# A recurrent attention kernel: the tail tokens' projections move from one batched stage into the steps, and the reloaded weight pieces change places in each group

## The chip, the core and the metric

The kernel runs on one core of one Trainium2 chip. The metric is the device time of one execution in microseconds (us). The core has five engines that run beside each other: TensorE (PE, matrix products; its weight loads appear as PEld), VectorE (DVE), ScalarE (ACT), GpSimd (POOL) and SyncE (SP, which only issues transfers). Weights come from the chip's memory (HBM) through 16 DMA engines into the on-chip memory SBUF; PE writes its results to eight banks of PSUM.

## What is computed

A sequence of 2048 tokens of width 1024 is cut into 64 segments of 32 tokens. Segment after segment, 8 memory tokens are put in front, the 40 tokens pass through attention with 32 heads of width 128, and the first 8 rows of the result are the memory of the next segment. So the segments form a chain. A gated feed-forward network works on all tokens, and a gate g mixes both.

```python
def _A_ref(x, mem0, Wq, Wk, Wv, Wo, seg_len):
    ...
    mem = mem0
    for s in range(n_seg):
        xs = x[:, s * seg_len:(s + 1) * seg_len, :].copy()
        h = jnp.concatenate([mem, xs], axis=1)
        q = jnp.einsum('btd,dhe->bhte', h, Wq)
        k = jnp.einsum('btd,dhe->bhte', h, Wk)
        v = jnp.einsum('btd,dhe->bhte', h, Wv)
        scores = jnp.einsum('bhqe,bhke->bhqk', q, k) * scale
        scores = jnp.where(mask[None, None], scores, -1000000000.0)
        p = _softmax(scores, axis=-1)
        o = jnp.einsum('bhqk,bhke->bhqe', p, v)
        o = jnp.einsum('bhte,hed->btd', o, Wo)
        mem = o[:, :M, :].copy()
        outs.append(o[:, M:, :])
...
g = _sigmoid((x * gate_w).sum(-1, keepdims=True))
b = _gelu(x @ w_gate) * (x @ w_up) @ w_down
return g * a + (1 - g) * b
```

## The kernel before

**Stages.** A first stage prepares tokens and projects the tail tokens; 64 steps follow, one a segment; then the output projection of the tail tokens (L854 to L874) and the feed-forward network (from L876), neither of which changes.

**Front and tail tokens.** A segment has 8 memory tokens and 32 new ones. A step puts the 8 memory tokens and the first 24 new ones (`NR = 24`) into one tile `hT` of 32 columns. The other 8 (`NB = 8`), the *tail tokens*, do not depend on the chain, so their q, k and v can be computed ahead. Before the change the first stage does so for all 512 tail tokens at once (L481 to L545): their transposed rows `xrT` go against all of Wk, Wq and Wv in products of 512 columns, and the results go to the scratch tensors `qk_scr` and `v_scr` in HBM. Each step reads its part back: `qkr` (L474) twice, once for each half of the heads, and `vB` (L478) once; `put_rest` (L777) copies `qkr` beside the front tokens in `kT` and `qT`.

**Weights.** Wq, Wk, Wv and Wo are 64 pieces of 512 KB: matrix m, half r of the heads, and i = 0 to 7. SBUF has 50 slots (`sl`) for them, so 36 pieces stay and 14 slots are *paired*: the two halves' pieces of the same m and i share one slot (`PAIRS`, L301: 3 for k, 3 for q, 4 for v, 4 for o). When a step has used the piece of one half, `spent` (L354) has SP fetch the other half's piece (L347), which the same step needs later. The next step takes the halves in the other order, so it starts with the pieces that are there. That is 14 fetches, 7.34 MB, in each step.

**A step** (L784 to L849) walks through eight groups of eight pieces in the order k0, q0, v0, k1, q1, o0, v1, o1 (`ORDER`, L293), where 0 is the half taken first. Within a group the pieces go in the order 0 to 7. `proj` (L749) issues 4 products of 128x512 for a piece of k, q or v (L758) and 8 of 128x256 for a piece of o (L770). What else happens is written into the same order by `on(...)`, by group and place: ACT copies a group's PSUM bank out (`evac`, L663), PE transposes it (`trans`, L670), `scores` (L689) and the softmax on DVE and ACT follow, `attend` (L720) multiplies with v, and its results `oT` feed the pieces of o. At the end of a step ACT copies the bank of o to `a_bf` (L832), PE transposes it (L836), and DVE writes the new memory tokens into the next `hT` (L839), after which the next step's k0 can start. `hT` has two buffers, and the next one's new tokens are loaded at place 5 of k0 (L808).

**Who orders what.** Each engine works off its own list in the order of the code, and waits are on semaphores. All fetches are in SP's list, all small reads and stores of the steps in POOL's.

Of the kernel before, what the change touches and what calls it, by code (L numbers as in the profile page):

```python
# [195 lines left out]
def bass_gated_mix__memory_aug_recurrent_mem_tr__geglu_ffn__prompt_kernel(  # L196
# [34 lines left out]
    with ExitStack() as es:  # L231
# [6 lines left out]
        NRT = NSEG * NB  # L238
        NBK = (NRT + 127) // 128
# [3 lines left out]
        qk_scr = nc.dram_tensor("qk_scr", [128, NSEG, 4, 128], BF16)  # L243
        v_scr = nc.dram_tensor("v_scr", [NSEG, NB, 16, 2, 128], BF16)
# [23 lines left out]
        hT = [al(f"hT{i}", [128, KC, 32]) for i in range(2)]  # L268
# [8 lines left out]
        vA = al("vA", [128, 4, 128], at=tok.off)  # L277
# [5 lines left out]
        a_bf = al("a_bf", [128, 256], at=oT.off)  # L283
# [7 lines left out]
        QUADS = (("k", 0), ("q", 0), ("k", 1), ("q", 1), ("v", 0), ("v", 1))  # L291
        pos = [(m, r, kc) for m, r in QUADS for kc in range(KC)] + [("o", r, i) for r in range(2) for i in range(8)]
        ORDER = (("k", 0), ("q", 0), ("v", 0), ("k", 1), ("q", 1), ("o", 0), ("v", 1), ("o", 1))  # L293
        walk = [(m, r, i) for m, r in ORDER for i in range(8)]
        assert len(pos) == 64

        def at_step(p, s):
            m, r, i = (pos if s < 0 else walk)[p]
            return (m, r ^ (s % 2), i)

        PAIRS = {"k": (1, 3, 5), "q": (0, 2, 5), "v": (0, 2, 4, 6), "o": (0, 2, 4, 6)}  # L301
# [12 lines left out]
        for s_ in [-1] + list(range(NSEG)):  # L314
            for p in range(48 if s_ < 0 else 64):
                k = at_step(p, s_)
                if s_ < 0 and k[0] == "v" and paired(k) and k[1] == 1:
                    continue
                uses[home[k]].append(k)
# [48 lines left out]
        for g in range(4):  # L368
# [11 lines left out]
        xrT = al("xrT", [128, KC, NRT])  # L380
        stq = [al(f"stq{i}", [128, max(NSEG, 64), 128]) for i in range(2)]
        xq = [al(f"xq{i}", [128, 4, KC, SEG]) for i in range(2)]
        assert cur[0] <= top

        tmpv = {k: al(f"tmpv{k[2]}", [128, 2048], at=stq[0].off + PIECE * n)
                for n, k in enumerate(("v", 1, i) for i in PAIRS["v"])}
        assert len(tmpv) * PIECE <= 2 * stq[0].nb
        cur[0] = slots[home["v", 0, 0]].off
        px = [al(f"px{i}", [128, D]) for i in range(min(NT, 16))]
        gwb = al("gwb", [128, D])  # L390
        gp = al("gp", [128, D], FP32, at=kT.off)
# [34 lines left out]
        for b in range(NBK):  # L426
# [6 lines left out]
            if b + 2 < NBK:  # L433
                rest_t.append(load_rest(b + 2))
# [553 lines left out]
```

## Time and profile before

| | us |
|---|---|
| three runs, median (lowest to highest) | 2736.53 (2732.96 to 2737.52) |
| the profiled execution's own time | 2737.58 |
| its span, first to last instruction | 2735.8 |
| PE busy over the span | 2236.5 (82%) |
| DVE / ACT / POOL busy | 900.9 / 540.3 / 437.9 |
| HBM traffic | 611.60 MB read, 30.41 MB written |

A row of a table by stretches gives the stretch, each engine's busy time with its number of instructions, the TensorE clock that was granted (1.00 is full speed), the mean busy share of the 16 DMA engines, and what they moved in GB/s. A row of the list of waits names the waiting instruction, whom it waited for, the total, how often, and the longest. A row of a timeline has start, length, engine, line, operation, output and inputs, shape, count, and in brackets the idle time before it with what ended it. A row of the DMA issues has the number of transfers, the size of each, and the median time from issue to landing. Instructions of one kind that follow each other are merged in a timeline.

### The profile page before, as it was taken

The numbers are of one execution on the slowest core, as the hardware profiler recorded it, in microseconds if no ns is written. First come the engines' busy times: TensorE is split into PE (matmuls) and PEld (weight loads), VectorE is DVE, ScalarE is ACT, GpSimd is POOL, SyncE is SP. The second block draws the span as 40 slices with busy tenths as digits, with TensorE's granted clock in tenths as the row PEclk, the third lists the DMA queues.
The fourth block names the chain that finished last, engine by engine and source line by source line (L and its number), as shares of the span: only waits on it lengthen the run. The fifth ranks groups of instructions, "written<-read, shape, count | busy, mean of one in ns | idle before, by whom it ended". The sixth has DMA issues, their size and how long they took to land.

```text
span 2735.8 us, 71514 instructions
## 1 busy us (share of the span) xinstructions
PE 2236.5 (82%) x32250; PEld 1046.5 (38%) x32294; DVE 900.9 (33%) x2089; ACT 540.3 (20%) x1129; POOL 437.9 (16%) x931
## 2 busy tenths in 40 slices
PE   7896777777777777777777777777878999999998
PEld 3442333333333333333333333333335444444443
DVE  1422233232333233323323333233230544445262
ACT  1211111121211121212112112112120312213030
POOL 1401222222122221222212212212210000000000
PEclk9998988899888899988888888889799999999999
DMA  8678787787877778878778787778788343250705
GB/s 307 181 209 318 253 280 267 262 293 251 293 270 264 278 260 282 282 252 285 263 258 285 256 286 281 242 275 283 241 293 288 131 150 112 85 177 15 247 1 200
DMA packets 293745, 646.78 MB, mean 236 GB/s; under 512 B 76728, under 2 KB 87992, under 8 KB 293440
## 3 DMA queue, kind: packets, MB, share of 16 engines
q1 hardware_dynamic: 237040, 594.63, 61.3%
q0 software_dynamic: 15360, 25.29, 3.8%
q10 hardware_dynamic: 41040, 22.29, 2.8%
q8 instruction: 254, 4.16, 0.6%
q14 instruction: 51, 0.42, 0.1%
HBM read 611.60 MB, written 30.41 MB: 235 GB/s over the span
## 4 chain that ended last, share of the span: by engine, by line
PE 49%; DMA 39%; DVE 5%; ACT 3%; issue 2%; SPq 1%; ACTq 1%; POOL 1%; POOLq 0%
DMA sl<-in_A_Wq_dram 23%; PE pb L758 14%; DMA sl<-in_A_Wo_dram 13%; PE pb L905 12%; PE pb L770 7%; PE pb L942 6%; PE pb L673 2%; PE pb L864 2%; PE pb L529 2%; PE pb L501 2%; DMA wd<-in_B_w_down_dram 2%; ACT tok L656 1%; ACT a_bf L656 1%; SPq L347 1%; PE pb L836 1%
## 5 line engine op out<-in xcount | busy, mean ns | idle before, releaser
L758 PE MATMUL pb<-sl,hT 128*32 128x512 bf16 x12288 | 905.2, 422 | 211.1 <-DMA sl<-in_A_Wk_dram 96.5
L758 PEld LDWEIGHTS pb<-sl,hT 128*32 128x32 bf16 x12288 | 309.7, 101 | 603.2 <-issue 159.9
L770 PE MATMUL pb<-sl,oT 128*32 128x256 bf16 x8192 | 346.6, 311 | 78.4 <-DMA sl<-in_A_Wo_dram 49.3
L770 PEld LDWEIGHTS pb<-sl,oT 128*32 128x32 bf16 x8192 | 223.4, 107 | 155.0 <-issue 91.3
L656 ACT ACTIVATE tok<-pb 128x512 bf16<-128x512 f32 x256 | 153.4, 599 | 397.7 <-PE pb L758 392.7
L905 PE MATMUL pb<-xT,wg 128*128 128x512 bf16 x896 | 211.8, 380 | 8.4 <-DVE GT L921 8.4
L741 POOL COPY oRc<-oT 128x128 bf16<-128x128 bf16 x128 | 96.0, 750 | 764.3 <-DVE oT L659 764.3
L905 PE MATMUL pb<-xT,wu 128*128 128x512 bf16 x896 | 211.7, 379 | 0.0
L942 PE MATMUL pb<-wd,GT 128*128 128x512 bf16 x876 | 193.9, 380 | 9.5 <-DMA wd<-in_B_w_down_dram 8.3
L659 DVE COPY kT<-pb 128x512 bf16<-128x512 bf16 x128 | 54.4, 425 | 337.8 <-PE pb L673 309.7
L659 DVE CAST oT<-pb 128x160 bf16<-128x160 f32 x256 | 71.3, 320 | 263.6 <-PE pb L732 263.6
L656 ACT ACTIVATE oT<-pb 128x160 bf16<-128x160 f32 x256 | 63.8, 301 | 425.0 <-PE pb L732 425.0
L704 ACT ACTIVATE E<-pb 128x320 bf16<-128x320 f32 x128 | 55.9, 437 | 417.9 <-DVE pb L703 417.9
L905 PEld LDWEIGHTS pb<-xT,wg 128*128 128x128 bf16 x896 | 86.8, 98 | 116.5 <-DVE GT L921 12.8
L942 PEld LDWEIGHTS pb<-wd,GT 128*128 128x128 bf16 x896 | 86.7, 98 | 116.7 <-DMA wd<-in_B_w_down_dram 13.2
L913 ACT ACTIVATE s<-pb 128x512 f32<-128x512 f32 x112 | 66.8, 596 | 323.0 <-PE pb L905 303.5
L727 PE MATMUL pb<-tA,vA 32*128 32x40 bf16 x2048 | 37.3, 185 | 112.7 <-DVE tB L717 112.7
L905 PEld LDWEIGHTS pb<-xT,wu 128*128 128x128 bf16 x896 | 87.5, 98 | 105.8
L914 DVE SCALAR_TENSOR_TENSOR tp<-s,pb 128x512 f32<-128x512 f32 x112 | 77.0, 687 | 136.7 <-ACT s L913 136.6
L501 PE MATMUL pb<-xrT,sl 128*128 128x512 bf16 x499 | 117.1, 390 | 5.2 <-DMA sl<-in_A_Wq_dram 2.5
L673 PE MATMUL pb<-ident,tok 128*128 128x128 bf16 x1024 | 111.6, 238 | 8.9 <-ACT tok L656 2.6
L673 PEld LDWEIGHTS pb<-ident,tok 128*128 128x128 bf16 x1024 | 63.6, 104 | 136.1 <-ACT tok L656 121.3
(76 smaller groups left out, 1821.3 us busy)
## 6 DMA issues: line engine op xcount, KB each, us to landing
sl<-in_A_Wv_dram SPq DMA_DIRECT2D x268, 512.0 KB, 11.4
sl<-in_A_Wo_dram SPq DMA_DIRECT2D x268, 512.0 KB, 6.4
sl<-in_A_Wk_dram SPq DMA_DIRECT2D x208, 512.0 KB, 7.1
sl<-in_A_Wq_dram SPq DMA_DIRECT2D x208, 512.0 KB, 9.5
wd<-in_B_w_down_dram SPq DMA_DIRECT2D x56, 1024.0 KB, 5.7
qk_scr<-stq ACTq DMA_DIRECT2D x4, 2048.0 KB, 18.3
qkr<-qk_scr POOLq DMA_DIRECT2D x128, 64.0 KB, 4.8
wg<-in_B_w_gate_dram SPq DMA_DIRECT2D x3, 1792.0 KB, 15.9
```

Of the source, the lines that this page charges most:

```text
L501: ins = e.matmul(PB[b][:, 0:NRT], lhsT=w8[kc][:, c:c + 128], rhs=xrT[:, kc, :], start=(kc == 0), stop=(kc == KC - 1))
L656: op("act", lambda e: e.activation(o, i, ACTF.Copy), rd=rd, wr=wr)
L659: op("dve", lambda e: e.tensor_copy(o, i), rd=rd, wr=wr)
L673: ins = e.transpose(PBV[TT][:, j * 128:(j + 1) * 128], tok[:, j * 128:(j + 1) * 128], ident[:, :])
L704: op("act", lambda e: e.activation(E8[:, :, :].rearrange("p a c -> p (a c)"), PB[SS][:, 0:320], ACTF.Exp, scale=scale), rd=[BK(SS)], wr=[E ...
L741: op("pool", lambda e: e.tensor_copy(oRc[:, :, 16 * u:16 * u + 16].rearrange("p c x -> p x c"), oT[:, :, :, 32:40].rearrange("p g j c -> p ...
L758: ins = e.matmul(PB[bk][32 * g:32 * g + 32, :], lhsT=h[:, i, :], rhs=w[:, g * 512:(g + 1) * 512], start=(i == 0), stop=(i == KC - 1))
L770: ins = e.matmul(PB[XO][32 * g:32 * g + 32, 0:256], lhsT=oT[:, gp_, 2 * jj + hh, 0:32], rhs=w[:, c:c + 256], start=(r == 0 and i == 0 and ...
L905: ins = e.matmul(PB[bk][:, 0:FB], lhsT=w[:, kc, cc:cc + 128], rhs=xT[:, :, :, kc, :].rearrange("p t i c -> p (t i) c"), start=(kc == 0), s ...
L913: op("act", lambda e, hg=hg: e.activation(s1[:, :], hg, ACTF.Square, scale=SQ), rd=[BK(bg)], wr=[s1.r()])
L914: op("dve", lambda e, hg=hg, t=t: e.scalar_tensor_tensor(out=t[:, :], in0=s1[:, :], scalar=1.0, in1=hg, op0=ALU.add, op1=ALU.mult), rd=[BK ...
L942: ins = e.matmul(PB[bank[2 * k + hf]][:, :], lhsT=GT[:, j, tb * 128:(tb + 1) * 128], rhs=w[:, jj, hf * 512:(hf + 1) * 512], start=(j == 0) ...
```

## The change

The batched stage is gone. The first stage now only transposes the tokens, 16 tiles of 128, and writes beside `xq_scr` a second scratch `xr_scr` with the tail tokens of each group of four segments: 4 x 8 = 32 columns, as many as `hT` has. The tile `hR` holds one such group. A *fill* is the projection of a group's 32 tail tokens with one half of Wk, Wq or Wv: eight pieces of 4 products, as in a step. A group of four segments needs six fills, and in four consecutive steps two, two, one and one of them are done for the group ahead (table `FILL`). They use pieces that are in their slots at that time, so they fetch no weights. The results go to `qk_scr` and `v_scr`. Step 0 does the fills of group 0 itself, as its pieces arrive, and one of group 1.

```diff
-        hT = [al(f"hT{i}", [128, KC, 32]) for i in range(2)]
+        hT = al("hT", [128, KC, 32])
+        hR = al("hR", [128, KC, 32])
-        vA = al("vA", [128, 4, 128], at=tok.off)
+        vA = al("vA", [128, 4, 128], at=oT.off)
-        a_bf = al("a_bf", [128, 256], at=oT.off)
+        a_bf = al("a_bf", [128, 256], at=qT.off)
+        stage = {n: al(n + "S", [128, 512], at=t.off) for n, t in (("k", kT), ("q", qT), ("o", oT))}
+        def seq(m, r):
+            p = [i for i in range(8) if i in PAIRS[m]]
+            f = [i for i in range(8) if i not in p]
+            return p + f if r == 0 else f + p
-        walk = [(m, r, i) for m, r in ORDER for i in range(8)]
+        walk = [(m, r, i) for m, r in ORDER for i in seq(m, r)]
...
+            if T > 0:
+                op("act", lambda e: e.dma_start(xr_scr[T], to.rearrange("p k i c -> p (k i c)")),
...
+        def fill(m, u, b, h=hR):
+            ks = [(m, u, i) for i in range(8)]
...
+                    for g in range(4):
+                        ins = e.matmul(PB[b][32 * g:32 * g + 32, :], lhsT=h[:, k[2], :], rhs=w[:, g * 512:(g + 1) * 512],
+                                       start=(n == 0), stop=(n == 7))
...
+        def fill_evac(m, u, G, b, st):
+            st = stage[st]
+            if m == "v":
+                act_copy(st[:, :], PB[b][:, :], [BK(b)], [st.r()])
+                for g in range(4):
+                    op("pool", lambda e, g=g: e.dma_start(
+                        v_scr[4 * G:4 * G + 4, :, 4 * g:4 * g + 4, u, :].rearrange("s i j c -> (s i) j c"),
...
+            else:
+                act_copy(tok[:, :], PB[b][:, :], [BK(b)], [tok.r()])
+        def fill_put(m, u, G, st):
+            if m == "v":
+                return
...
+                    ins = e.transpose(PBV[TT][:, j * 128:(j + 1) * 128], tok[:, j * 128:(j + 1) * 128], ident[:, :])
...
+            op("pool", lambda e: e.dma_start(qk_scr[:, 4 * G:4 * G + 4, m4, :], st[:, :].rearrange("p (i y) -> p i y", i=4)),
+               rd=[st.r()], wr=[("D", "qk", G, m4)], lane="fq")
...
+        FILL = ((("k", 1), ("q", 1)), (("q", 0), ("v", 0)), (("v", 1),), (("k", 0),))
...
-            on("k", 0, 5, lambda: load_h(s + 1) if not last else None)
+                on("k", 0, 5, lambda: load_v(s))
-            on("v", 0, 7, lambda: scores())
+            on("k", 1, 0, lambda: scores())
-            on("q", 1, 4, lambda: attend(ua))
+                on("q", 1, 5, lambda: attend(ua))
-            on("o", 0, 7, lambda: scores())
+            on("v", 1, 0, lambda: scores())
+            two = len(fl) > 1
+            n1, n2, n3 = (3, 3, 8) if two else (0, 3, 2)
+            on("v", 1, 0, some(f1, n1))
+            on("o", 1, 0, lambda: load_h(s + 1) if not last else None)
             on("o", 1, 0, lambda: evac(bko["v", 1], vA, "act"))
+            on("o", 1, 0, some(f1, n2))
             on("o", 1, 0, lambda: attend(ub))
-            on("o", 1, 0, lambda: load_v(s + 1) if not last else None)
+            on("o", 1, 0, some(f1, n3))
+            on("o", 1, 0, o_store)
...
             act_copy(a_bf[:, :], PB[XO][:, 0:256], [BK(XO)], [a_bf.r()])
+            fb = f2 if two else f1
+            run(fb, 4 if two else 2)
...
+            run(fb)
```

`seq` puts a group's paired pieces first in the half taken first and last in the half taken second. Three memory places are shared anew: `vA` no longer lies on `tok` but on `oT`, `a_bf` on `qT`, and the staging tiles of the fills (`kS`, `qS`, `oS`) on `kT`, `qT` and `oT`.

The change moves rows on **PE at the end of a step** and the start of the next one. `sl` tiles are weight pieces with their slot numbers (the numbers of before are two or three lower), `oT`, `hT`, `hR` the tokens' side of a product, `pb` a PSUM bank. Before, from the middle of o1 to the third piece of k0 of the next step:

```order
L770 MATMUL pb<-sl_113,oT 32x256 x8
L770 MATMUL pb<-sl_114,oT 32x256 x8
L770 MATMUL pb<-sl_116,oT 32x256 x8
L770 MATMUL pb<-sl_117,oT 32x256 x8
L836 MATMUL pb<-ident,a_bf 128x128 x2
L758 MATMUL pb<-sl_69,hT_53 32x512 x4
L758 MATMUL pb<-sl_71,hT_53 32x512 x4
L758 MATMUL pb<-sl_72,hT_53 32x512 x4
```

Now, the same place in a step with two fills:

```order
L674 MATMUL pb<-sl_119,oT 32x256 x8
L689 MATMUL pb<-sl_85,hR 32x512 x4
L689 MATMUL pb<-sl_87,hR 32x512 x4
L689 MATMUL pb<-sl_88,hR 32x512 x4
L689 MATMUL pb<-sl_90,hR 32x512 x4
L836 MATMUL pb<-ident,a_bf 128x128 x2
L689 MATMUL pb<-sl_92,hR 32x512 x4
L689 MATMUL pb<-sl_93,hR 32x512 x4
L689 MATMUL pb<-sl_95,hR 32x512 x4
L689 MATMUL pb<-sl_97,hR 32x512 x4
L662 MATMUL pb<-sl_74,hT 32x512 x4
L662 MATMUL pb<-sl_77,hT 32x512 x4
```

Four pieces of the second fill now stand between the last piece of o and the transposes of `a_bf`, and four between these and k0 (two and one in a step with one fill). The last piece of o is a paired one (`sl_119`), where it was an unpaired one (`sl_117`), and k0 begins with a paired one (`sl_74`), where it was an unpaired one (`sl_69`).

On **POOL**, from the last `oRc` copy of a step to the first memset of the next, the small transfers change places. Before:

```order
L741 COPY oRc<-oT 128x16x8
L478 DMA vB<-v_scr 128x1x256
L778 COPY kT<-qkr 128x16x8
L778 COPY qT<-qkr 128x16x8
L845 DMA a_scr<-a_bf 4x32x256
L847 DMA o_scr<-oRc 128x256
L474 DMA qkr<-qk_scr 128x256
L469 DMA hT_53<-xq_scr 128x256
L701 MEMSET pB 128x144
```

Now, behind a step with two fills, whose second is one of v:

```order
L433 DMA hT<-xq_scr 128x256
L646 COPY oRc<-oT 128x16x8
L817 DMA o_scr<-oRc 128x256
L719 DMA qk_scr<-kS 128x4x128
L846 DMA a_scr<-a_bf 4x32x256
L700 DMA v_scr<-oS 32x4x128 x4
L723 COPY kT<-qkr 128x16x8
L723 COPY qT<-qkr 128x16x8
L442 DMA qkr<-qk_scr 128x256
L446 DMA vB<-v_scr 128x1x256
L606 MEMSET pB 128x144
```

The load of `hT` and the store of `oRc` moved ahead of the step's end, the load of `vB` behind the start of the next step, and the fills' stores (`qk_scr`, `v_scr`) came in.

On **SP** at the start of the program the token tiles 8 to 15 (`px`, whose buffers are used a second time) now stand ahead of the Wv pieces:

```order
L351 DMA sl_94<-in_A_Wq_dram 128x2048
L351 DMA sl_96<-in_A_Wq_dram 128x2048
L403 DMA px_122<-in_A_x_dram 128x1024
L403 DMA px_123<-in_A_x_dram 128x1024
L403 DMA px_124<-in_A_x_dram 128x1024
L403 DMA px_125<-in_A_x_dram 128x1024
L403 DMA px_126<-in_A_x_dram 128x1024
L403 DMA px_127<-in_A_x_dram 128x1024
L403 DMA px_128<-in_A_x_dram 128x1024
L403 DMA px_129<-in_A_x_dram 128x1024
L351 DMA sl_98<-in_A_Wv_dram 128x2048
```

Before, each tile had a buffer of its own, and their loads stood between the pieces of the first two groups.

More of the change, by code (lines that the diff above doesn't have):

```diff
@@ L383, in bass_gated_mix__memory_aug_recurrent_mem_tr__geglu_ffn__prompt_kernel @@
+        dl = al("dl", [128, NT], FP32)
         assert cur[0] <= top
[L385 to L391, printed above, removed]
-        pr = [al(f"pr{i}", [128, D], at=kT.off + 2048 * i) for i in range(2)]
```

330 lines of the change are left out of this document (150 added, 180 removed).

## The prediction

> **What bounds the kernel now.** I first read the table by stretches, cut at the start of the wait for step 0's first reloaded piece, at the end of step 0, and at the end of the last step.
>
> ```profile
> 0.00:219.50 219.50, 190.87 (x1059) 90.02 (x1077) 62.31 (x96) 42.35 (x72) 40.67 (x43) 0.97 0.75 238
> 219.50:248.60 29.10, 16.10 (x301) 6.87 (x301) 4.88 (x14) 3.47 (x9) 3.67 (x9) 0.69 0.86 325
> 248.60:2080.00 1831.40, 1400.24 (x28009) 657.22 (x28011) 557.47 (x1575) 354.71 (x821) 393.60 (x879) 0.88 0.78 272
> 2080.00:2736.00 656.00, 629.31 (x2883) 292.35 (x2906) 276.26 (x404) 139.78 (x228) 0.00 (x0) 1.00 0.38 132
> L656 ACT ACTIVATE a_bf<-pb x64: 383/383/384, 248.2 to 2062.2; 128x256 bf16<-128x256 f32 x64
> ```
>
> The first stage is PE's: 190.87 of 219.50 us busy. In the steps neither PE (1400 of 1831 us) nor the DMA engines (0.78) are full. `a_bf` ends each step: 64 of them, the first at 248.2, the last at 2062.2, so a step takes 1814.0/63 = 28.79 us. Behind the last `a_bf` lie 2737.58 - 2062.6 = 675.0 us that the change leaves alone.
>
> Next the list of PE's waits within the steps:
>
> ```profile
> PE pb L727 <- DVE tB L717: 110.9, 63, 1.8
> PE pb L758 <- DMA sl<-in_A_Wq_dram: 92.0, 122, 2.8
> PE pb L758 <- DMA sl<-in_A_Wk_dram: 83.4, 104, 2.2
> PE pb L770 <- DMA sl<-in_A_Wo_dram: 49.3, 82, 2.2
> PE pb L836 <- ACT a_bf L656: 30.5, 63, 0.5
> PE pb L770 <- ACT oT L656: 26.8, 63, 0.4
> PE pb L758 <- DVE hT L839: 17.9, 63, 0.3
> ```
>
> More than half is for fetched pieces: 224.7 us, 3.6 a step. The rest, 186 us, is the chain of the data: softmax, the copies of `oT`, the end of a step. To see whether the fetches wait in a full queue or come late, I cut one step, from its k0 to the next k0:
>
> ```profile
> 1051.77:1054.00 2.23, 2.23 (x44) 1.15 (x48) 0.00 (x0) 0.27 (x1) 2.03 (x4) 1.00 0.30 85
> 1054.00:1068.00 14.00, 11.39 (x213) 4.27 (x205) 4.75 (x13) 3.25 (x8) 1.58 (x5) 0.88 0.99 353
> 1068.00:1074.00 6.00, 4.15 (x122) 2.58 (x118) 3.35 (x9) 1.22 (x3) 0.73 (x2) 1.00 0.85 278
> 1074.00:1078.00 4.00, 2.40 (x68) 1.30 (x68) 0.56 (x2) 0.50 (x2) 1.58 (x4) 0.87 0.66 248
> 1078.00:1080.29 2.29, 1.44 (x19) 0.68 (x19) 0.19 (x1) 0.38 (x1) 0.44 (x1) 0.50 0.00 0
> ...
> 1094.00:1096.00 2.00, 0.73 (x28) 0.28 (x24) 0.56 (x2) 0.99 (x3) 1.03 (x2) 1.00 1.03 420
> ```
>
> The DMA engines are full for 14 us (0.99, 353 GB/s), dip while the pieces of o are asked for, and stand still at the end of the step. So a step is one long queue of 14 pieces, then a tail in which nothing can be fetched because nothing has been used yet. (The last row is two of the best microseconds of the step after it.) The timeline of the same step shows both ends:
>
> ```profile
> 1052.43 1.30 SPq L347 DMA_DIRECT2D sl<-in_A_Wk_dram  x3
> 1067.80 3.49 SPq L347 DMA_DIRECT2D sl<-in_A_Wo_dram  x4
> 1051.77 2.77 PE L758 MATMUL pb<-sl,hT 128*32 128x512 bf16 x48 [0.28 <-DVE hT L839]
> 1054.48 0.40 PE L673 MATMUL pb<-ident,tok 128*128 128x128 bf16 x4
> 1068.57 1.06 PE L770 MATMUL pb<-sl,oT 128*32 128x256 bf16 x32
> 1070.24 1.93 PE L758 MATMUL pb<-sl,hT 128*32 128x512 bf16 x32
> 1078.08 1.05 PE L770 MATMUL pb<-sl,oT 128*32 128x256 bf16 x16 [0.47 <-DMA sl<-in_A_Wo_dram]
> 1079.61 0.40 PE L836 MATMUL pb<-ident,a_bf 128*128 128x128 bf16 x2 [0.49 <-ACT a_bf L656]
> 1080.29 4.46 PE L758 MATMUL pb<-sl,hT 128*32 128x512 bf16 x48 [0.28 <-DVE hT L839]
> ```
>
> 48 products are 12 pieces: 2.77/12 = 0.231 us a piece at clock 1.00, and 4.46/12 = 0.372 us where the clock was half; a piece of o takes 1.06/4 = 0.27, four transpositions 0.40.
>
> **The change, part 1: the start of the program.** The batched projections go, and with them a first stage as long as PE's work. What remains before `a_bf` of step 0 is loading. I count what must land before step 0 can leave its fills: 38 pieces of k, q and v, 12 of o and the 10 reloaded ones of k, q and v, 60 x 0.524 = 31.5 MB; tokens in 4.2 MB, their transposed form out 4.2, the tail tokens' scratch 1.0, the rest (gate vector, seven fills' stores, small reads) 1.6: 42.4 MB. At the full queue's 353 GB/s that is 120.1 us.
>
> ```profile
> pr<-in_A_x_dram SPq DMA_DIRECT2D x4, 256.0 KB, 3.7
> sl<-in_A_Wv_dram SPq DMA_DIRECT2D x268, 512.0 KB, 11.4
> qk_scr<-stq ACTq DMA_DIRECT2D x4, 2048.0 KB, 18.3
> qkr<-qk_scr POOLq DMA_DIRECT2D x128, 64.0 KB, 4.8
> DMA to landing us min/median/max: 3.5/8.5/15.7
> DMA to landing us min/median/max: 2.9/5.8/7.8
> L456 POOL TENSOR_TENSOR gp<-px,gwb 128x1024 f32<-128x1024 bf16 x16 | 34.0, 2123 | 82.8 <-DVE dl L458 63.5 <-DMA px<-in_A_x_dram 19.3
> L458 DVE TENSOR_REDUCE dl<-gp 128x1 f32<-128x1024 f32 x16 | 19.5, 1218 | 15.8 <-POOL gp L456 15.8
> ```
>
> (The two rows without a name are those of the weight pieces and of `hT`.) In front come 3.7 us until a first tile lands. Behind come the k1 and q1 pieces, a transposition and the first piece of o, 16 x 0.231 + 0.40 + 0.27 = 4.4 us; then the four last pieces of o, asked for only now: 3.5 us for one alone (the least of the first unnamed row) and 3 x 0.524/0.353 = 4.5 us for the others; then 0.7 us. Sum: 3.7 + 120.1 + 4.4 + 8.0 + 0.7 = 136.9 us, against 248.6 at the end of step 0's `a_bf` before: **-111.7 us**. The gate's pass (2.12 us on POOL, then 1.22 on DVE, one tile after the other, 16 x 3.4 = 54 us) holds the SP list at tiles 8 to 15 until about 36 us; until then 16 pieces and 15 tiles, 12 MB, are under way with 3 MB of stores, 42 us of queue, so I cost it at nothing; without that cover it is 10 us. The fills' round trips through HBM (some 10 us from store to `qkr`, at twice 4.8) lie under the same queue. Bounds: 118 us at the 420 GB/s of the best row, and 157 at step 0's own 325 GB/s with the 10 us.
>
> **Part 2: one step.** Per step, against 28.79:
> - First fetch after one piece of k0 instead of two: -0.23.
> - The dip: SP needs 3.49 us for the o fetches because the pieces 0, 2, 4, 6 lie between others; now all four are first. At 0.85 of 6 us the dip is worth 0.9: -0.9, between 0 and 1.4 (with part of the next row).
> - At the end one piece of o, not two, stands behind the last landing: -0.3 (half of 1.05 at half clock, 0.26 at full).
> - The load of `hT` and the store of `oRc` leave the first microseconds, in which the k pieces ask for the engines, and go beside the o pieces; `vB` comes in. Two transfers of 64 KB at 353 GB/s are 0.4: -0.4, between 0 and -1.0.
> - The fills' stores and `hR`: (6 x 128 + 64) KB for four steps, 0.213 MB a step, in pieces of 256 bytes. At 353 GB/s 0.6 us of the full queue; at the pace of the one row with such pieces, 2048 KB in 18.3 us, 1.85. That row's transfers shared the queue with weights, so I take +0.85, nearer the low end.
> - The tail: with two fills, 4 pieces stand where PE waited 0.49 for `a_bf`, and 4 where it waited 0.28 for `hT`: +1.07 at full clock, +2.21 at half. With one fill (2 and 1 pieces) it is 0 to +0.35. Half of the steps have two: +0.7, between 0.55 and 1.3.
> - All other fill pieces (8 or 5 ahead of o1) lie in the wait for `tB` (1.76 a step), that for `oT` (0.43) and that for o pieces. In a step with one fill 3 x 0.231 cover part of `tB` only. Their four transpositions (of k and q) for four steps, 0.40 each, fall in waits for pieces. 0, as long as the o pieces land last; without that cover up to 1.85.
> - `hT` with one buffer: its load may start when the last v1 product has read it, 1072.17 in this step, 8.1 us before the next k0; it lands in 5.8 and DVE and its semaphore take 0.5. 0, with 1.8 us to spare.
> - `vB`, issued some 5 us into a step, is needed at the fifth piece of q1, where q pieces are waited for anyway: 0.
>
> Sum: -0.23 - 0.9 - 0.3 - 0.4 + 0.85 + 0.7 = **-0.28 a step**, 63 x 0.28 = 17.6 us. All terms at their ends: -2.0 to +2.4.
>
> So PE receives 96 fills x 8 x 0.231 = 177 us of work, nearly what the first stage had, and the steps hardly grow, since the 431 us in which PE stood still take it, while the queue of fetches stays as long.
>
> Sum against the profiled execution: 2737.58 - 111.7 - 17.6 = **2608 us**. The median of the three runs is 1 us below that execution, which I leave out.
>
> On the granted clock: 0.88 over the steps, 0.50 in the last row of the step. The Trainium skill, "TensorE: Matmul & The Clock Gate", section "Why this matters for your kernels", says that idle gaps of PE of more than about 3 us put it back to half clock; the trace agrees in kind, since half clock comes here behind the stretches of waits, although the longest single wait in the list is 2.8 us. By that rule the fills would keep PE warm, and its 1400 us at 0.88 would be 1232 at 1.00. I give this no term, because a step ends with a fetch and not with PE; it is part of the first rival's chance.
>
> **The rivals.**
> - *The queue has slack that only PE's order kept it from using.* For it: 0.70, 0.15 and 0.34 of the first, third and fourth stretch are idle. Against: the 14 us at 0.99. It gives the favourable ends of all terms, -2.0 a step: 2737.58 - 111.7 - 126 = 2500.
> - *The stores in 256-byte pieces and half-clock fills in the tail eat the gain.* For it: 18.3 us for 2 MB, and half clock in the last row. Against: 18.3 was measured in a shared queue. With +1.85 for the stores a step is 0.72 longer than before: 2608 + 63 x 1.0 = 2671. The Trainium skill, "DMA: Bandwidth & Descriptors", section "Specifications", wants at least 512 B a transfer for line rate and says that smaller ones are read, modified and written. That speaks against moving these stores into the stage where the queue is the limit. The 18.3 us agree with a slow store but can't tell that cause from queueing.
> - *Slower than before: `hT` lands too late.* Its load now competes with four pieces of o, and with it waits the whole next step. In favour: Wv pieces, queued behind others, take 11.4 us; against: a 64 KB load on POOL's own queue never took over 7.8. Each us beyond 7.6 is a us of every step. From 1.8 + 0.28 = 2.1 us more, a landing after 9.7, the gain of the start is gone; at 11.4 it is 63 x 3.8 = 239 more: 2847.
> - *The change doesn't do what it says at the start,* since loads hold each other up as they did in the first stage (238 GB/s over it): 42.4 MB then take 178 us, 58 more: 2666.
>
> **How the numbers follow.** Forecast (steps between 1.1 shorter and 0.3 longer than before) 0.50; queue with slack 0.17; slow stores 0.19; `hT` late 0.06; long start 0.08. Range: the first stage's -19 and +20 with steps 1.2 shorter and 1.1 longer than forecast, not added in full: 2512 to 2700. It leaves out most of the first rival, the third, and the worst of the second. A measurement of this kernel tells 0.2% (5 us) from no change. Faster by more than that: 0.93, all cases but the third rival and a rest; within: 0.01; slower: 0.06.
>
> **What would show it.** Right: the first `a_bf` ends near 137; the distance of `a_bf` is about 28.5, longer in steps with two fills than in those with one; the wait for `tB` is mostly gone, and PE's waits for DMA move to o1; the dip in the DMA share closes; PE busy in the steps rises by some 180 us. Wrong: DVE's copy into `hT` waits for the transfer of `hT`; the DMA share in the steps stays at 0.78 while steps get shorter or longer; or the first `a_bf` is past 157.

## The result and the profile after

| | before | after |
|---|---|---|
| median of 4 runs (lowest to highest), us | 2734.74 (2716.38 to 2737.52) | 2508.94 (2505.66 to 2514.83) |
| ratio, 95% interval | | 0.919 (0.9145 to 0.9235) |
| the profiled execution's own time / span, us | 2737.58 / 2735.8 | 2514.83 / 2512.9 |

The changed kernel takes 8.1% less time. The table by stretches of its profile, cut where step 0's last fetches are asked for, and at the ends of the first and of the last `a_bf`, and the row of `a_bf`:

```profile
0.00:110.00 110.00, 38.96 (x461) 21.77 (x465) 35.48 (x67) 15.95 (x28) 44.89 (x49) 0.90 0.99 378
110.00:138.30 28.30, 22.04 (x413) 10.69 (x409) 5.61 (x15) 5.50 (x11) 9.04 (x17) 0.84 0.36 115
138.30:1843.80 1705.50, 1416.97 (x31012) 731.06 (x31004) 582.12 (x1633) 410.72 (x907) 532.49 (x1073) 0.97 0.83 296
1843.80:2513.00 669.20, 641.37 (x2944) 298.44 (x2944) 276.12 (x404) 140.38 (x230) 0.73 (x1) 0.99 0.40 138
L561 ACT ACTIVATE a_bf<-pb x64: 384/384/386, 137.9 to 1843.4; 128x256 bf16<-128x256 f32 x64
```

The first `a_bf` ends at 138.3 instead of 248.6: 110.3 us less. From there to the last one are 1705.5 us instead of 1814.0, so a step takes (1843.4 - 137.9)/63 = 27.07 us instead of 28.79: 63 x 1.72 = 108.5 us less. What lies behind the last `a_bf` is 669.1 us instead of 673.2. These three make up the whole 222.9 us between the spans. So the two halves of the gain are alike in size, and the second was forecast at 17.6.

PE's waits in the steps (from 139 to 1844 us):

```profile
PE pb L632 <- DVE tB L622: 92.3, 95, 2.0
PE pb L632 <- DMA vB<-v_scr: 45.6, 23, 4.0
PE pb L674 <- DMA sl<-in_A_Wo_dram: 43.6, 55, 1.8
PE pb L662 <- DMA sl<-in_A_Wq_dram: 35.1, 47, 2.3
PE pb L662 <- DMA sl<-in_A_Wk_dram: 15.9, 20, 1.6
PE pb L662 <- ACT vA L561: 12.4, 19, 1.2
PE pb L662 <- DMA sl<-in_A_Wv_dram: 8.7, 17, 0.9
```

The waits for pieces fell from 224.7 us to 43.6 + 35.1 + 15.9 + 8.7 = 103.3; of those for k and q, 175.4 before, 51.0 are left. The wait for `tB` is still there, 95 times instead of 63. Two rows are new: for `vB` and for `vA`. The waits for `a_bf`, `oT` and `hT`, 75.2 us before, are nearly all filled.

One step, of the same segment as the one shown before (there 28.52 us, here 27.03), cut in the same manner:

```profile
903.91:906.14 2.23, 1.96 (x36) 0.88 (x32) 0.42 (x1) 0.60 (x1) 0.20 (x1) 1.00 0.40 100
906.14:918.00 11.86, 10.34 (x229) 5.20 (x221) 4.75 (x13) 3.61 (x8) 3.84 (x9) 1.00 1.00 362
918.00:924.00 6.00, 5.12 (x135) 2.83 (x131) 3.35 (x9) 0.64 (x3) 0.76 (x2) 1.00 1.03 390
924.00:928.61 4.61, 3.78 (x98) 2.05 (x90) 0.98 (x3) 1.69 (x4) 2.61 (x4) 1.00 0.65 232
928.61:930.94 2.33, 2.29 (x42) 1.10 (x46) 0.19 (x1) 0.38 (x1) 0.74 (x1) 1.00 0.26 63
```

The dip is gone: while o's pieces are asked for the DMA engines are full (1.03, 390 GB/s; before 0.85 and 278). PE works through the tail at full clock. The timeline of that step shows how:

```profile
904.35 1.54 SPq L351 DMA_DIRECT2D sl<-in_A_Wk_dram  x3
912.34 0.60 ACT L561 ACTIVATE vA<-pb 128x512 bf16<-128x512 f32 x1 [2.92 <-DMA qk_scr<-oS]
917.82 2.66 SPq L351 DMA_DIRECT2D sl<-in_A_Wo_dram  x4
928.65 0.40 PE L674 MATMUL pb<-sl,oT 128*32 128x256 bf16 x8 [0.26 <-DMA sl<-in_A_Wo_dram]
928.88 1.04 PE L689 MATMUL pb<-sl,hR 128*32 128x512 bf16 x16
929.85 0.28 PE L836 MATMUL pb<-ident,a_bf 128*128 128x128 bf16 x2
930.07 1.05 PE L689 MATMUL pb<-sl,hR 128*32 128x512 bf16 x16
930.94 1.68 PE L662 MATMUL pb<-sl,hT 128*32 128x512 bf16 x28
```

The fetches of o start 13.9 us into the step (16.0 before) and take 2.66 us to issue (3.49 before). One piece of o is left behind the last landing, then come four fill pieces, the transposition, four more, and k0.

Averaged over 58 steps (issue and landing of each of the 14 fetches in the trace, counted from k0): the first fetch lands at 4.83 us (before 6.94), the tenth at 19.27 (19.7), the first of o is asked for at 14.8 (17.0), and the last of o lands at 25.03 (26.63). From there to `a_bf` are 0.62 us (1.12), and from `a_bf` to the next k0 1.40 (1.04; with two fills 1.84, with one 1.02).

### The profile page after: what moved, and what is told of

Read it like the earlier page. It is cut to its first block, busy times and chain, and to the rows that moved or that the text cites. A ratio compares the mean times of both kernels' runs of the same rounds, so it can differ in the third digit from the quotient of the medians.

```text
span 2512.9 us, 76509 instructions
## 1 busy us (share of the span) xinstructions
PE 2119.3 (84%) x34822; PEld 1062.0 (42%) x34822; DVE 899.3 (36%) x2119; ACT 572.5 (23%) x1175; POOL 587.1 (23%) x1139
## 4 chain that ended last, share of the span: by engine, by line
PE 44%; DMA 42%; DVE 5%; issue 3%; ACT 3%; POOL 2%; SPq 0%; ACTq 0%; POOLq 0%
DMA sl<-in_A_Wq_dram 17%; DMA sl<-in_A_Wo_dram 14%; PE pb L909 13%; PE pb L674 7%; PE pb L662 7%; PE pb L946 6%; PE pb L689 4%; DMA vB<-v_scr 3%; DMA qk_scr<-oS 3%; PE pb L868 2%; PE pb L578 2%; DMA wd<-in_B_w_down_dram 2%; DMA xr_scr<-xr 1%; ACT tok L561 1%; POOL gp L428 1%
## 5 line engine op out<-in xcount | busy, mean ns | idle before, releaser
L662 PE MATMUL pb<-sl,hT 128*32 128x512 bf16 x12288 | 794.3, 386 | 76.6 <-DMA sl<-in_A_Wq_dram 35.1
L662 PEld LDWEIGHTS pb<-sl,hT 128*32 128x32 bf16 x12288 | 322.2, 97 | 394.5 <-DMA sl<-in_A_Wq_dram 52.3
L674 PE MATMUL pb<-sl,oT 128*32 128x256 bf16 x8192 | 307.1, 292 | 51.1 <-DMA sl<-in_A_Wo_dram 43.6
L561 ACT ACTIVATE tok<-pb 128x512 bf16<-128x512 f32 x320 | 191.3, 598 | 370.3 <-PE pb L662 316.4
L674 PEld LDWEIGHTS pb<-sl,oT 128*32 128x32 bf16 x8192 | 210.8, 103 | 132.8 <-DMA sl<-in_A_Wo_dram 61.9
L689 PE MATMUL pb<-sl,hR 128*32 128x512 bf16 x3072 | 226.8, 393 | 7.4 <-issue 4.0
L632 PE MATMUL pb<-tA,vA 32*128 32x40 bf16 x2048 | 36.7, 179 | 143.3 <-DVE tB L622 92.3
L564 DVE COPY qT<-pb 128x512 bf16<-128x512 bf16 x128 | 54.4, 425 | 253.7 <-PE pb L578 240.4
L561 ACT ACTIVATE vA<-pb 128x512 bf16<-128x512 f32 x128 | 76.4, 597 | 279.2 <-DMA v_scr<-oS 106.5
L918 DVE SCALAR_TENSOR_TENSOR tp<-s,pb 128x512 f32<-128x512 f32 x112 | 77.0, 687 | 131.9 <-ACT s L917 131.8
L607 DVE TENSOR_REDUCE st<-pb 128x8 f32<-128x320 f32 x128 | 63.0, 492 | 170.2 <-PE pb L602 170.2
```

What stands on the lines that cost most here:

```text
L561: op("act", lambda e: e.activation(o, i, ACTF.Copy), rd=rd, wr=wr)
L564: op("dve", lambda e: e.tensor_copy(o, i), rd=rd, wr=wr)
L607: op("dve", lambda e: e.tensor_reduce(nm, sS, AX.X, ALU.max, negate=True), rd=[BK(SS)], wr=[st8.r(0, 8)])
L662: ins = e.matmul(PB[bk][32 * g:32 * g + 32, :], lhsT=h[:, i, :], rhs=w[:, g * 512:(g + 1) * 512], start=(p % 8 == 0), stop=(p % 8 == 7))
L674: ins = e.matmul(PB[XO][32 * g:32 * g + 32, 0:256], lhsT=oT[:, gp_, 2 * jj + hh, 0:32], rhs=w[:, c:c + 256], start=(r == 0 and p % 8 == 0 ...
L689: ins = e.matmul(PB[b][32 * g:32 * g + 32, :], lhsT=h[:, k[2], :], rhs=w[:, g * 512:(g + 1) * 512], start=(n == 0), stop=(n == 7))
```

## The experiments

Theories on the 1.44 us by which a step beat the forecast: (1) the new order of the pieces gains more than costed; (2) the fills and their stores cost less than costed, perhaps because they keep PE's clock up; (3) both. Each run has one profile, and its mean step is the distance of the first and last `a_bf` over 63. Single steps scatter by 0.7 to 0.9 us about it, and a profile is of one execution of four, which lie 4 to 24 us apart: e1's is its fastest, 9 us under its median, e4's and e11's are their slowest, 10 and 13 us above. The last column therefore adds (median - profiled time)/63 to the mean step, an estimate that puts the whole distance into the steps; the kernel before comes to 28.75 so, the changed one to 26.98. (The kernel before, run again beside each group of these, had medians from 2723.9 to 2732.2 us.) Differences under about 0.2 us a step aren't told apart here, unless both columns and a second pair of runs agree.

| run | what it is | median, us | ratio to before, 95% | mean step, us | the same, to the median |
|---|---|---|---|---|---|
| e1 | changed kernel, natural order | 2625.4 | 0.957 to 0.963 | 28.70 | 28.84 |
| e2 | kernel before, new order alone | 2610.6 | 0.950 to 0.959 | 26.85 | 26.76 |
| e5 | new order only in the half taken first | 2581.4 | 0.942 to 0.948 | 28.16 | 28.12 |
| e6 | new order only in the half taken second | 2549.0 | 0.931 to 0.936 | 27.66 | 27.60 |
| e11 | of e6, only o1 | 2609.6 | 0.953 to 0.964 | 28.82 | 28.62 |
| e12 | of e6, only k1, q1 and v1 | 2560.3 | 0.933 to 0.945 | 27.86 | 27.84 |
| e3 | changed kernel without fills in the steps | 2513.4 | 0.917 to 0.923 | 27.09 | 27.08 |
| e7 | fills without their stores | 2515.0 | 0.917 to 0.924 | 27.05 | 27.04 |
| e4 | `vB` loaded at the end of a step | 2492.1 | 0.908 to 0.915 | 26.79 | 26.63 |
| e8 | e4, fills moved out of the tail | 2482.9 | 0.906 to 0.912 | 26.57 | 26.47 |
| e9 | e8 without fills | 2472.2 | 0.900 to 0.908 | 26.44 | 26.41 |
| e10 | e8, v's fills dealt out anew | 2482.4 | 0.903 to 0.912 | 26.57 | 26.55 |

### The order of the pieces: e1, e2

e1, in the changed kernel:

```diff
-            return p + f if r == 0 else f + p
+            return list(range(8))
```

> The changed kernel with one part undone: every group walks its pieces 0 to 7 again. Fills, buffers and small transfers stay as changed. Theory 'order' (the step is a queue of 14 fetches, and the new order starts it earlier, closes its dip and leaves one piece behind the last landing; 1.43 us a step by the forecast's terms): the distance of a_bf goes from 27.07 to about 28.5, total about 2605. Rival 'warm PE' (the fills keep PE's clock up, and that made the steps shorter): steps stay near 27.1 at a clock near 0.97, total about 2515.

e2, in the kernel before, with `seq` and the group's first and last product marked by place instead of by piece:

```diff
-        walk = [(m, r, i) for m, r in ORDER for i in range(8)]
+        walk = [(m, r, i) for m, r in ORDER for i in seq(m, r)]
```

> The kernel before with only the new order of pieces: batched stage, two hT buffers and all small transfers as before. Theory 'order': a step goes from 28.79 to about 27.4, total about 2648, first a_bf still near 248. Rival 'warm PE': steps stay at about 28.8, total about 2736.

With the old order the changed kernel's step is 28.70 us, no different from before. The new order alone makes the step of the kernel before 26.85 us, 1.94 less. So nearly all of the steps' gain is the order of the pieces (1.94 alone, 28.70 - 27.07 = 1.63 in the changed kernel, 1.86 by the last column), and everything else together adds 0.2 to what the order alone reaches. The forecast had 1.43 for it. A warmer PE isn't the cause: from 300 to 1800 us the granted clock is 0.93 in e1, whose steps are long, and 0.92 in e2, whose steps are as short as the changed kernel's at 0.97.

### Which half of the order: e5, e6

```diff
-            return p + f if r == 0 else f + p
+            return p + f if r == 0 else list(range(8))      # e5
+            return list(range(8)) if r == 0 else f + p      # e6
```

> The changed kernel with half of the new order: paired pieces first in the half taken first, and places 0 to 7 in the half taken second. By the forecast's terms (first fetch 0.23 and dip 0.9 of the 1.43) a step is 1.13 shorter than the 28.70 with the old order: 27.57, total about 2546. Rival 'use late' (what counts is that a paired piece is used late, not that it is fetched early): little gain, about 28.4, total about 2598.

> The changed kernel with the other half of the new order: places 0 to 7 in the half taken first, paired pieces last in the half taken second. By the forecast's terms (one piece instead of two behind the last landing, 0.3) 28.40, total about 2598. Rival 'use late': about 27.6, total about 2546. If the two halves add up, this gain and that of the run with the other half make 1.63 together; if less or more, one half needs the other.

Against e1, paired pieces first (k0, q0, v0, o0) gain 0.54 us a step, paired pieces last (k1, q1, v1, o1) gain 1.04; together 1.58 of the 1.63 (by the last column 0.72 and 1.24 for 1.86). The forecast had it the other way round: 0.23 + 0.9 = 1.13 for the first half, 0.3 for the second.

### Where the second half's gain arises: e11, e12

```diff
-            return list(range(8)) if r == 0 else f + p
+            return f + p if r == 1 and m == "o" else list(range(8))      # e11
+            return f + p if r == 1 and m != "o" else list(range(8))      # e12
```

> The changed kernel with the natural order 0 to 7 everywhere but in o1, where the paired pieces come last. Beside e1 (natural everywhere: mean step 28.70 us) and e6 (paired last in k1, q1, v1 and o1: 27.66 us), it splits the 1.04 us of the order's second half. The forecast's own reading, only the one piece less behind the last landing counts: 28.4 us (-0.3), and e12 28.70. Theory A, in k1, q1 and v1 an unlanded piece stood ahead of resident ones and held PE, so PE reached o0 late and asked for o's pieces late: here 28.3 to 28.5 us, and e12 27.8 to 28.1. Theory B, all of it is o1, where four resident pieces run before the paired ones land: here 27.6 to 27.9 us, and e12 28.6 to 28.8.

> The other part: paired pieces last in k1, q1 and v1, natural order in o1 and in the half taken first. The forecast's own reading: mean step 28.70 us, as e1. Theory A: 27.8 to 28.1 us, the o fetches issued earlier against the step's start than in e1, and PE's waits for Wk and Wq pieces down by a third or more. Theory B: 28.6 to 28.8 us. If this one and e11 add up to much less than 1.04 us, the two parts hide behind each other: then each alone meets the other's wait.

k1, q1 and v1 gain 0.84 (1.00 by the last column). What o1 gains alone, e11 doesn't tell: its mean step is 0.12 longer than e1's, but its median is 15.8 us lower. Beside k1, q1 and v1 it gains 0.20 (e12 against e6; 0.24 by the last column, 0.22 for e11), near the forecast's 0.3, and the trace shows how: `a_bf` starts 0.62 us behind the last landing in e6, and 0.89 in e12. So the forecast's own term, one piece less behind the last landing, is there, but it is the smaller part of what paid, and the theory that all was o1 falls. PE's waits from 300 to 1800 us, of e1:

```profile
PE pb L662 <- DMA sl<-in_A_Wq_dram: 90.1, 99, 3.3
PE pb L662 <- DMA sl<-in_A_Wk_dram: 57.6, 54, 2.7
PE pb L632 <- DVE tB L622: 53.5, 51, 1.4
PE pb L674 <- DMA sl<-in_A_Wo_dram: 29.2, 47, 2.1
...
PE pb L632 <- DMA vB<-v_scr: 1.4, 1, 1.4
```

and of e12:

```profile
PE pb L632 <- DVE tB L622: 60.9, 71, 1.7
PE pb L662 <- DMA sl<-in_A_Wq_dram: 48.4, 61, 2.4
PE pb L674 <- DMA sl<-in_A_Wo_dram: 48.1, 72, 1.4
PE pb L662 <- DMA sl<-in_A_Wk_dram: 40.0, 42, 2.4
PE pb L632 <- DMA vB<-v_scr: 35.7, 20, 4.0
```

PE takes its list in order. In the old order the second place of k1 and the first of q1 held a piece still on its way (`PAIRS` has 1 for k and 0 for q), and the resident pieces behind it waited with PE: 147.7 us for k and q in e1, 88.4 in e12 over the same 1500 us. (v1 changed along with them and wasn't run by itself.) PE now comes to o0 earlier, so SP asks for o's pieces earlier: at 16.7 us after k0 in e1, at 15.4 in e12. The last of o lands at 26.3 in e1, and at 25.6 in e12. In e11 it is 26.7: nothing made that landing earlier there.

The last row of each shows the price: reaching the first half's products with v earlier, in q1, PE finds `vB` not there, 35.7 us instead of 1.4.

### `vB`: e4

```diff
-            else:
-                on("k", 0, 5, lambda: load_v(s))
...
+            on("o", 1, 0, lambda: load_v(s + 1) if not last else None)
```

> The changed kernel with one transfer moved back: vB of the next step is loaded behind the second attend of a step, as before the change, not at place 5 of k0. PE waits 45.6 us for vB in the changed kernel, 0.72 a step. If this wait sets the step: steps at about 26.4, total about 2470. If the q pieces or the o fetches, which land in the queue's own time, take its place: steps within 0.2 of 27.07, total 2500 to 2515, and PE's waits for DMA of the pieces grow by about the same 45 us.

The step falls from 27.07 to 26.79 us. How long the load takes, from issue to landing, in the changed kernel and then in e4:

```profile
L446 POOL DMA_DIRECT2D vB<-v_scr x65: 545/549/558, 101.2 to 1821.6; - x65
DMA to landing us min/median/max: 5.0/6.3/7.8
```

```profile
L446 POOL DMA_DIRECT2D vB<-v_scr x65: 544/551/557, 101.6 to 1796.0; - x65
DMA to landing us min/median/max: 2.0/2.1/5.7
```

Issued at place 5 of k0, the 64 KB share the DMA engines with the pieces of k, q and v: the engines' mean busy share from issue to landing is 1.00. At the end of the step before it is 0.29. The place that the change gave up is worth 0.28 us a step, 17 us between the medians.

### The fills and their stores: e3, e7

e3 leaves the fills of the steps out and reads the tail projections of the first four segments in place of all others'; e7 computes the fills but doesn't store them, and reads the same.

```diff
-            fl = [(m, u, G) for m, u in FILL[s % 4]] if G < NG else []      # e3
+            fl = []
...
-                for g in range(4):                                          # e7: v's stores; q's and k's likewise
+                for g in range(4 if G == 0 else 0):
```

> The changed kernel without any fill in the steps, with neither their products nor their stores nor the loads of hR; every step reads the tail tokens' projections of group 0, so that its reads are as large as before. Forecast's prices (0.85 for the stores, 0.7 for the tail of a step): steps at about 25.5, total about 2417. Rival 'slack' (the fills lie in time that is idle anyway, except the 0.79 us that the two-fill tails are longer): about 26.7, total about 2490. Rival 'warm PE': PE's clock falls back towards 0.88 and steps become longer than 27.07, total above 2515.

> The changed kernel with all fills' products, copies and transpositions in the steps, but without their stores to qk_scr and v_scr; the steps read the projections of group 0. Without fills at all steps were 27.09, with all 27.07. If that is nothing plus nothing, steps stay within 0.15 of 27.07, total 2505 to 2520. If the stores cost and PE's warmer clock gives it back, steps fall: by 0.85 (the forecast's price) to 26.2, total about 2460; by 0.3 to 26.8, total about 2492.

Without fills a step takes 27.09 us, without their stores 27.05, with both 27.07: both seem to cost nothing, where the forecast had 0.7 + 0.85. But part of this is cover. The waits for `vB` from 300 to 1800 us, first of e3, then of e7, then of the changed kernel:

```profile
PE pb L632 <- DMA vB<-v_scr: 76.5, 41, 4.2
```

```profile
PE pb L632 <- DMA vB<-v_scr: 71.8, 34, 3.8
```

```profile
PE pb L632 <- DMA vB<-v_scr: 38.3, 19, 4.0
```

Where the fills or their stores are left out, PE meets the late `vB` twice as long. So these two runs can't give the fills' price; it has to be taken where `vB` is not late.

### The fills with `vB` out of the way: e8, e9, e10

e8 is e4 with most of the fill pieces taken from behind the last o piece to the waits for `tB` and `oT` and ahead of o1's paired pieces (`n1`, `n2`, `n3` are the pieces at the start of v1 and in these two waits; two stay where PE waits for `a_bf`, and with two fills one behind it):

```diff
-            n1, n2, n3 = (3, 3, 8) if two else (0, 3, 2)
+            n1, n2, n3 = (3, 5, 3) if two else (0, 5, 1)
+            fb = f2 if two else f1
...
-            on("o", 1, 0, some(f1, n3))
+            on("o", 1, 0, some(fb, n3))
+            if two:
+                on("o", 1, 4, some(f2, 2))
...
-            run(fb, 4 if two else 2)
+            run(fb, 2)
```

> The kernel with vB loaded early, and most fill pieces taken out of the end of a step: in steps with two fills 5 of them in the wait for tB, 3 in that for oT, 2 ahead of the paired o pieces, 2 beside the copy of a_bf and 1 behind it (before 3, 2, 0, 4 and 4); in steps with one, 5, 1, 0, 2 and 0. If the longer tail of the steps with two fills (1.83 us from a_bf to k0 against 1.04) is paid in full, 30 of them lose up to 0.75 each: 2492 goes to about 2470. If these pieces only move PE's wait (the last o piece lands later after k0 by as much), the total stays at 2485 to 2497.

e9 is e8 with `fl = []` and the reads of e3, so nothing of the above is left in it but e4's load of `vB`:

> The kernel with vB fetched early (e4, and so e8) without the fills, their stores and hR inside the steps; it leaves out the tail projections of the segments behind the first four and reads those of the first four in their place. Against e8 (2482.9 us, mean step 26.57 us, clock 0.972 and 0.23 of a step's PE time on fills). Theory A, fills lie wholly in PE's waits: mean step 26.45 to 26.65, median 2473 to 2489 us. Theory B, the fills keep PE's granted clock up and so pay for themselves: clock under 0.945 and a mean step of 26.75 us or more, 2494 us or more. Theory C, fills still cost what the remaining one or two behind the last o piece cost (0.3 to 0.4 us a step): mean step 26.25 or less, 2463 us or less.

e10:

```diff
-        FILL = ((("k", 1), ("q", 1)), (("q", 0), ("v", 0)), (("v", 1),), (("k", 0),))
+        FILL = ((("v", 1), ("k", 1)), (("v", 0), ("q", 0)), (("q", 1),), (("k", 0),))
```

> e8 with the fills dealt out anew over a group of four steps: v goes first of two and is stored from the other staging tile early in o1, so that vA, which shares its bytes with oS, is no longer written behind v's stores. Theory A, ACT's wait at vA (88 us on v's stores in e8, a release that PE waited 7.8 us for) is on the path: the row of vA behind v_scr goes and the mean step falls by 0.1 to 0.4 us, to 26.2 to 26.5 us, 2458 to 2477 us. Theory B, vA is evacuated ahead of its need and the wait is ACT's own slack: mean step 26.5 to 26.65 us, 2478 to 2488 us. Theory C, the copy of v and its stores early in o1 hold back ACT's copies of oT or hT's fetch on the same queues: mean step over 26.7 us, over 2491 us.

All that belongs to the fills costs 26.79 - 26.44 = 0.35 us a step (e4 against e9; 0.22 by the last column), of which e8 takes back 0.22 (0.16). e8's first `a_bf` starts at 140.1 us and e9's at 131.9, so of the 15.4 us between the profiled executions about half, 0.13 x 63 = 8, is the steps'; the medians are 10.7 apart. What is left of the fills' price in e8 isn't told from nothing. Here are both over the same 1500 us of steps, e8 and then e9:

```profile
300.00:1800.00 1500.00, 1272.44 (x27763) 655.86 (x27759) 521.10 (x1463) 365.96 (x813) 478.19 (x962) 0.97 0.84 301
```

```profile
300.00:1800.00 1500.00, 1169.34 (x25165) 606.34 (x25153) 502.97 (x1422) 330.84 (x738) 371.48 (x791) 0.92 0.83 296
```

With the fills the granted clock is 0.97 instead of 0.92, and the step is not shorter (26.57 against 26.44). This refutes the theory that they pay for themselves by a warm PE. Nor do the stores delay the queue: the last piece of o lands 24.68 us after k0 in e4, with stores, and 24.74 in e9, without.

e10 was to show whether ACT's copy into `vA`, which now lies on the staging tile `oS` and has to wait for the stores from it, is on the path. The step is as long as e8's, but the run doesn't settle it. ACT's wait for v's stores went and the one for the stores of q and k grew; PE's own wait for `vA` rose from 7.8 to 30.8 us, and other waits shrank by as much. Of e8:

```profile
ACT vA L561 <- DMA v_scr<-oS: 88.3, 25, 4.5
ACT vA L561 <- PE pb L662: 87.9, 66, 4.7
ACT vA L561 <- DMA qk_scr<-oS: 69.1, 21, 5.2
```

and of e10:

```profile
ACT vA L561 <- DMA qk_scr<-oS: 195.3, 51, 6.1
ACT vA L561 <- PE pb L662: 56.1, 62, 2.6
```

What is known is the bound from e9, which has no such waits: with everything else of the fills they are worth 0.13 us a step. A staging tile of their own was not tried. e8 and e10 are the fastest kernels here that do all of the work, 1% below the changed kernel.

## Why the prediction was right where it was, and what it mis-sized

**The time** is 2508.9 us against a forecast of 2608, which was counted from the profiled execution before; that of the changed kernel took 2514.8. The first lies 3 us below the range of 2512 to 2700, the second 3 us inside it, and both near the first rival's 2500. The sign, the start and the bound (the queue of fetches) were right; the size of one step was not. The case that had the chance of 0.50, steps between 1.1 shorter and 0.3 longer, did not come: they are 1.72 shorter, which is the first rival, at 0.17. The result is at the range's edge and not far outside it because the lower end takes in a part of that rival. Three slips of the text don't move the forecast: its range is nearly the full sum of its parts (-19 - 76 and 20 + 69), though it says that they aren't added in full; the step's terms at their upper ends come to some +2.6, not +2.4; and four runs of the kernel before lie from 2716 to 2738, wider than the 5 us that it gives as told from no change.

**The start of the program**: first `a_bf` at 138.3 us for 136.9. That it is so near is luck: two errors cancel in it. The full queue moved 378 GB/s, not 353, and was done near 110 us instead of 124; behind it PE had 22.0 of 28.3 us to work, the rest of step 0 and its fills, where the forecast had 13.1 us of a few pieces and landings. Long start is refuted.

**One step**, by differences of runs that follow each other from the kernel before to the changed one (so they add up by themselves):

| term | forecast | measured | to the medians | from |
|---|---|---|---|---|
| order of the pieces: first fetch, dip, o piece behind the last landing | -1.43 | -1.94 | -1.99 | e2 - before |
| `hT` and `oRc` out of the ramp (measured with all other edits but fills and order) | -0.4 | -0.41 | -0.35 | e9 - e2 |
| fills in the tail, their stores and `hR` | +1.55 | +0.35 | +0.22 | e4 - e9 |
| `vB` | 0 | +0.28 | +0.35 | changed kernel - e4 |
| sum | -0.28 | -1.72 | -1.77 | |

- *The order.* The mechanism named, fetches asked for earlier and closer together, is there: the dip closed, o's fetches start 2.2 us earlier. But the step that failed is what it was priced from: the half that is taken first, and of the half taken second only o1, at -0.3 (-0.20 between e12 and e6). k1, q1 and v1 have no term. The forecast missed that a piece on its way, standing ahead of resident ones in k1 and q1, holds the whole list; e12 shows that to be -0.84. The first half was over-sized: -0.54 by e5 (-0.72 by the last column) for -1.13, perhaps since as long as PE comes to o0 at 16.3 us (e5's mean) closer issues help little.
- *`hT` and `oRc`.* The size agrees, but e9 and e2 differ in more than these two transfers (one `hT` buffer, the softmax's place, the shared memory), so the cause is argued. For it: the first fetch lands at 5.62 us in e2 and at 5.05 in e9, the last of o at 25.21 and 24.76.
- *The fills.* The terms that failed are +0.85 and +0.7. The tail was costed between full and half clock, and the clock there is 1.00 in the step shown and 0.98 on the mean (before 0.78; from 1 us ahead of `a_bf` to k0): 1.84 - 1.04 = 0.80 us in steps with two fills, nothing in those with one, 0.4 on the mean. The price of the stores was taken between the full queue's (0.6) and that of the one row with 256-byte pieces (1.85), a row of a shared queue as the text itself said. Together they measure 0.35, so the stores seem to cost little or nothing; a run without stores alone, with `vB` early, was not made. The second rival is refuted. The Trainium skill, "DMA: Bandwidth & Descriptors", section "Specifications", asks for 512 B a transfer for line rate; the last landings of e4 and e9 above, 24.68 and 24.74, show no delay of the weight pieces from smaller ones at 0.213 MB a step, and don't test the rate of the stores themselves.
- *`vB` at nothing.* The cover named, q pieces that are waited for anyway at that place, was true in the old order (1.4 us of waiting for `vB` in e1) and taken away by the change's own new order (38.3 over the same stretch). Each edit was costed against the profile of before, not against the step as the other edits would leave it.
- *`hT` with one buffer at nothing*: right. All 63 waits of DVE's copy into `hT` end by PE's transposition, none by the load, and the third rival is refuted.
- *The clock without a term*: right, as far as e9 shows. The clock in the steps rose from 0.88 to 0.97, and still the steps end by fetches (`a_bf` starts 0.62 us behind the last landing); with the fills' work in them, the warm steps of e8 are no shorter than those of e9 at 0.92. What the clock alone would buy, without that work, no run shows. The Trainium skill, "TensorE: Matmul & The Clock Gate", section "Why this matters for your kernels", warns of idle gaps of PE over about 3 us between bursts, as they put the clock back to half. That limit doesn't separate these kernels: the longest wait is 2.8 us in the kernel before, at 0.88, and 4.0 in the changed one, at 0.97.

**Of the signs named**, the first `a_bf`, the closed dip and the row of waits moving to o's pieces came. The distance of `a_bf`, named at about 28.5, is 27.07. Steps with two fills are longer by 0.2 us only, and only if counted from k0 to k0 (27.35 and 27.05 against 26.84 and 27.09). From `a_bf` to `a_bf`, as the sign was put, they are shorter (26.56 and 27.10 against 27.66 and 27.06), as the pieces behind `a_bf` count to the next distance. The wait for `tB` did not go (92.3 us for 110.9); it changed its place. PE's rows of the products that wait for it, in one step of before:

```profile
1065.17 0.32 PE L727 MATMUL pb<-tA,vA 32*128 32x40 bf16 x16
1073.96 0.28 PE L727 MATMUL pb<-tA,vA 32*128 32x40 bf16 x16 [1.80 <-DVE tB L717]
```

and in two steps after, the first with two fills, the second with one:

```profile
915.35 0.27 PE L632 MATMUL pb<-tA,vA 32*128 32x40 bf16 x16 [1.02 <-DVE tB L622]
924.65 0.27 PE L632 MATMUL pb<-tA,vA 32*128 32x40 bf16 x16
943.38 0.27 PE L632 MATMUL pb<-tA,vA 32*128 32x40 bf16 x16 [1.10 <-DVE tB L622]
953.19 0.28 PE L632 MATMUL pb<-tA,vA 32*128 32x40 bf16 x16 [1.33 <-DVE tB L622]
```

At the second half's product two fills cover it, one covers a part, as forecast. At the first half's, where PE used to come late, it now comes early, has no fill to do there, and waits 1.0 us.

PE's busy time rose by 17 us, not 180. An estimate with the clock taken out: 1400.24 x 0.88 = 1232 and 1416.97 x 0.97 = 1374, a rise of 142 at full clock. The 180 also had all 96 fills in these steps; nine of them lie in step 0.

**The first rival**, that the queue has slack which PE's order kept from use, is what happened, with its price of -2.0 met by -1.72. The text had it, with the idle shares of 0.70, 0.15 and 0.34 that spoke for it, but as a case in which all small terms fall well, not as the mechanism that e12 shows.

## What to carry to other kernels

Where an engine takes its list in order and fetches are asked for as buffers are used, use first what frees a buffer for the next fetch, and put everything that is resident ahead of what is on its way, in every group and not only in the last: here both together were worth 1.94 of 28.79 us a step, and the second rule was the larger part. Cost each edit against the step as the others leave it; a cover that one edit names, another may remove. And price work put into waits by a run without it in which no other late transfer fills the gap.

## What the runs showed of the hardware

- The same 64 KB load took 6.3 us to land with the DMA engines full (share 1.00) and 2.1 with them at 0.29; PE of the changed kernel waited 4.0 us at the longest for it.
- The weight queue moved 378 GB/s over the first 110 us and 390 over 6 us of a step, more than the 353 taken as full.
- The granted clock over the steps stood at 0.88 before, at 0.92 in e9, at 0.93 in e1 and at 0.97 in the changed kernel and e8, and said nothing on which kernel is faster: e9, the shortest step of all, has no higher clock than e1, one of the longest.
